# The step behind an output block: second scores ahead of the weighted sums, and differences that end ten products before the block's end

## The chip, the cores and the metric

The kernel runs on one core of one Trainium2 chip. The metric is device microseconds from start to end. The kernel before took 1464.12 us (median of three runs, 1463.6 to 1466.82).

## The reference

Two attention branches read the same input x (2048 rows of 512) and are mixed by a gate. Everything is float32.

```python
g = sigmoid((x * gate_w).sum(-1, keepdims=True))
# branch A: 32 heads of 16, each row looks at 8 rows, 2 apart, behind it
logits = einsum("bhsd,bhswd->bhsw", q, kg) * scale      # masked before row 0
o_a    = einsum("bhsw,bhswd->bhsd", softmax(logits), vg)
# branch B: 32 query heads of 16, one key and one value head, all 2048 keys
scores = einsum("bhqd,bkd->bhqk", q, k) * 16 ** -0.5
o_b    = einsum("bhqk,bkd->bhqd", softmax(scores), v)
return g * (o_a @ A_wo) + (1 - g) * (o_b @ B_wo)
```

## The kernel before, in words

**Units and steps.** Branch B is 4 blocks of 512 queries by 8 groups of 4 heads, 32 units. A unit is 16 steps, one for each 128 keys, so there are 512 steps. Step s does three things. Two pairs of score products (`exp_pair(s, 0)` and `exp_pair(s, 1)`, L471, contraction 64, the two of a pair in the upper and the lower half of the array) fill a bank pair each, `pe0` and `pe1`. ScalarE turns each into 128x1024 exponentials (L477, tile `pexp`). And `weighted(s)` (L486) adds the weighted sums of the values into the bank `po`. A step in the loop issues the scores of s and the weighted sums of s - 1.

**Maxima.** A softmax needs its row maximum before its exponentials, so the maxima of a unit are made some units ahead: 2048 score products of 128x512 whose largest value VectorE takes. They are put wherever there is room, in three forms:

- a pair (`fill_pair`): two products into the bank pair `pm`, one reduction of 128x1024 (L350);
- a single (`fill_one`): one product into `ps` (also called m1) or `po`, one reduction of 128x512 (L362);
- a difference (`fill_diff`, L399, then `fill_sum`): one product with the difference of two key blocks into `pd0` or `pd1`, which ScalarE clamps at zero (L411, tile `dd`); then one product into `ps` or `po`, which VectorE adds to the clamped part and reduces in one instruction (L423). Two of the 2048 products are settled by it.

**Output blocks.** Three times in the loop, `out_phase` multiplies four rows of tiles of the finished branches by the output weights. Each product is split between the upper and the lower half of the array; two streams, one for each half, are issued side by side, and maxima go between them. While a block runs, the bank pair `pm` is split into `pd0` and `pd1`. The block's fourth output lies in `pe1`. At its end `out_store` copies it: ScalarE the upper half's sum (L685), then VectorE the lower half's (L686), both into the tile `two`; GpSimd adds the two (L692). Until both copies are done, `pe1` can take no new scores.

**Order.** Each engine works through its instructions in the order written. That order comes from a planner that runs while the kernel is built. It keeps a clock for each engine and a time at which each bank is free, and issues a filler if its bank is free within a slack. In `stream`, which plans a block, `closing` is true near the end: no new differences then. At the same point, once the first scores of step s are out, `rejoin` makes `pd0` and `pd1` the pair `pm` again, which takes the second scores of s (`exp_pair(s, 1, m2, "m2")`). The set `led` holds the three steps s that a block stood in; the step behind such a block has an order of its own.

The page's lines that this text speaks of, beside those above: L803 is the block's product, L643 and L645 prepare a row of tiles, L652 and L659 to L663 turn one, L689 copies an output inside the block.

Of the kernel before, what the change touches and what calls it, by code (L numbers as in the profile page):

```python
# [41 lines left out]
LEAD, M2S, M1S, MARGIN = 1.75, 0.5, 0.3, 0.12  # L42
# [6 lines left out]
def gated_mix_kernel(ctx, tc, xt, wa, wk, wq, wo_a, wo_b, out):  # L49
# [21 lines left out]
    m1 = pp.tile([P, 512], F32, name="ps")  # L71
    po = pp.tile([P, 512], F32, name="po")
    pp2, m2 = None, None
# [230 lines left out]
    free = {"m1": 0.0, "e0": 0.0, "e1": 0.0, "po": 0.0, "d0": 24.0, "d1": 24.0}  # L304
# [89 lines left out]
    def paired():  # L394
        return len(slots) > 1 and slots[0][3] % 2 == 0 and slots[0][3] // 2 in formed and slots[1] == slots[0][:3] + (slots[0][3] + 1,) and fillable()
# [20 lines left out]
    def room(b, slack):  # L416
        return len(pend[b]) < len(held[b]) and read_d[b][turn_of[b] % len(held[b])] <= clk["pe"] + slack

    def fill_sum(b, dst, key):
        v, pr, t, kc, k, ready = pend[b].pop(0)  # L420
        m = unit_tile(v)
        max_mm(dst, v, pr, t, kc + 1, b)
        got = nc.vector.tensor_tensor_reduce(held[b][k], dst, held[b][k], 1.0, -FMAX, ALU.add, ALU.max, m[:, b, pr, t, kc:kc + 1])  # L423
        free[key] = read_d[b][k] = after("dve", max(after("pe", 0, T_R) + T_LAT, ready), T_TTR) + 0.08
        mark(got, free[key])
        filled(v, 2)

    def fill_odd(b, dst, key):
        got = next((h for h in half if h[4] == b), None)
        if got is None:  # L430
            v, pr, t, kc = slots.pop(0)
            got = (v, pr, t, kc, b)
            half.append((v, pr, t, kc, 1 - b))
        else:
            half.remove(got)
        half.insert(0, got)
        fill_one(dst, key)
# [26 lines left out]
    pe, pexp, exped, homes = [], {}, {}, []  # L464
# [230 lines left out]
    def fits(key, slack=-MARGIN):  # L695
        return key in free and free[key] <= clk["pe"] + slack and not (wanted and key in ("d0", "d1"))

    def side_fill(b, closing):
        now = clk["pe"]
        dst, key = ((m1, "m1"), (po, "po"))[b]  # L700
        if pend[b]:
            if fits(key) and pend[b][0][5] <= now + 0.7 and clk["dve"] <= now + 1.5:
                return lambda: fill_sum(b, dst, key)
            if len(pend[b]) == len(held[b]):
                return None
        single = not pend[b] and fits(key) and clk["dve"] <= now + 1.4
        if any(h[4] == b for h in half):
            return (lambda: fill_odd(b, dst, key)) if single else None
        if todo[b] or paired() and len(todo[1 - b]) < 2:
            if fits(f"d{b}") and room(b, 1.2) and clk["act"] <= now + 2.2 and clk["dve"] <= now + 2.6 and not closing:  # L710
                return lambda: fill_diff(b, apart[b], f"d{b}")
            if todo[b] and single:
                return lambda: plain(b, dst, key)
        elif slots and fillable() and single and not paired():
            return lambda: fill_odd(b, dst, key)
        return None
# [8 lines left out]
    def plain(b, dst, key):  # L725
        if todo[b]:
            v, pr, t, kc = todo[b].pop(0)
            half.extend([(v, pr, t, kc, b), (v, pr, t, kc + 1, b)])
        fill_odd(b, dst, key)

    apart = []
# [9 lines left out]
    def stream(seq, mm, done, s):  # L741

        nonlocal pp2
        at, told = [0, 0], 0
        ready = free.pop("m2")
        pp2.release()
        pp2 = tc.alloc_tile_pool(name="parts", bufs=1, space=PSUM)
        if len(held[0]) < 2:
            more = p1x[0].tile([P, 2, 512], F32, name="dd2", tag="qx", bufs=1)
            for b in range(2):  # L750
                held[b].append(more[:, b])
                read_d[b].append(0.0)
        apart[:] = [pp2.tile([P, 512], F32, name=f"pd{k}") for k in range(2)]
        free["d0"] = free["d1"] = ready
        free["po"] = 1e9
        cl = [clk["pe"]] * 2
        while min(at) < len(seq) or any(pend):
            if free["po"] > 1e8 and min(at) > 3 and max(cl) > exped[s - 1] + 0.1:
                clk["pe"] = max(cl)
                weighted(s - 1)  # L760
                finish_a((s - 1) // NJ, nc.gpsimd)
                free["po"] = clk["dve"] + 0.1
                cl = [clk["pe"]] * 2
            if apart and max(at) > len(seq) - 6 and s in exped and max(free["d0"], free["d1"]) <= max(cl):
                clk["pe"] = max(cl)
                rejoin()
                exp_pair(s, 1, m2, "m2")
                cl = [clk["pe"]] * 2
            b = int(cl[1] < cl[0])
            clk["pe"] = cl[b]  # L770
            do = side_fill(b, max(at) > len(seq) - 6)
            if do:
                do()
                cl[b] += T_R
            elif at[b] < len(seq) and at[b] <= at[1 - b] + 2:
                dur = mm(b, seq[at[b]])
                cl[b] = clk["pe"] + dur
                at[b] += 1
            else:
                cl[b] += 0.07  # L780
            clk["pe"] = cl[b]
            while told < min(at):
                told += 1
                done(seq[told - 1])
        plain_todo()
        clk["pe"] = max(cl)
        if apart:
            rejoin()
            exp_pair(s, 1, m2, "m2")
# [93 lines left out]
    def fill_ready(key, slack):  # L883
        if fillable() and free[key] <= clk["pe"] + slack:
            clk["pe"] = max(clk["pe"], free[key])
            if key == "m1":
                fill_one()
            elif half and (not slots or half[0][0] < slots[0][0] or slots[0][0] >= len(stacked)):
                fill_one(m2[:, 0, :], "m2")
            elif slots:  # L890
                fill_pair(m2, "m2")
            return True
# [365 lines left out]
    outs, due, led = 0, [], set()  # L1258
    for s in range(NS + 1):
        u, kt = divmod(s, NJ)  # L1260
        if len(stacked) < NU and s >= max(2, 16 * (gone(len(stacked)) + 1)):
            stack(len(stacked))
        if s < NS and kt == 0 and u not in shifted:
            while u not in shifted:
                clk["pe"] += 0.5
                run_tasks()
                if u not in shifted and left.get(u, 1):
                    assert pause(4)
        v = min(x[0][0] for x in (half, slots, [(NU,)]) if x)
        need = left.get(v, NF // NU)  # L1270
        steps = 16 * v - 6 - s
        short = need - 2.8 * max(0, steps) if v < NU else 0
        lead = (NF - to_go()) / 64 - s / 16
        order = (0, "m2", "m1", 1) if s > 1 else (1, "m2", "m1", 0) if s else ()
        if s - 1 in led:
            order = (0, "m2", "m1", "po", 1)
        k, n = outs // 4, C - (outs >= NJ - 4)
        if outs == NJ - 4:
            if short > 0 and steps < 2:
                pause(short)  # L1280
        elif due or outs < NJ and outs // NH in done and kt == 15 and NHG * (k + 1) - 1 in shaped and (lead < LEAD or s >= 16 * (NHG * (k + 2) + 1) - 1):
            if not due:
                prepare(outs, n)
                due.append(n)
            else:
                out_phase(list(range(outs, outs + 4)), due.pop(), s)
                outs += 4
                led.add(s)
                order = ()
        elif short > 0 and steps < 2:  # L1290
            pause(short)

        for which in order:
            if which == "m2":
                if slots or half:
                    fill_ready("m2", M2S)
                else:
                    next(tail, None)
            elif which == "m1":
                if singles(s) and fill_ready("m1", M1S):  # L1300
                    owing[0] -= 1.0
            elif which == "po":
                weighted(s - 1)
            elif s < NS:
                exp_pair(s, which)
        if s - 1 in exped:
            weighted(s - 1)
            if kt == 0 and s < NS:
                finish_a(u - 1, nc.gpsimd)
        run_tasks()  # L1310
        run_pool()
# [79 lines left out]
```

## Time and profile before

| what | value |
|---|---|
| median of three runs | 1464.12 us |
| the profiled execution's own time | 1463.92 us |
| its span in the trace | 1462.1 us |
| TensorE busy | 1448.2 us (99%) |
| ScalarE busy | 1292.0 us (88%) |
| VectorE busy | 1141.9 us (78%) |
| GpSimd busy | 954.6 us (65%) |
| share of TensorE in the chain that ended last | 92% |
| output blocks | about 845 to 880, 1144 to 1176 and 1275 to 1308 us |

In rows of instructions in order of time, the columns are the start, the time from the first start to the last end, engine, line, operation, tiles with shapes and how many; in brackets the idle time of that engine before the row, and what ended it. A matmul of 512 columns lasts about 0.39 us, but the next starts after 0.12 to 0.24 us, so how long TensorE needs for a piece of work is read from start to start. In rows of stretches of time each engine has its busy microseconds and count, and PEclk is the granted clock, 1.00 at full speed.

### The profile page before, as it was taken

How to read it: one execution, taken by the hardware profiler on the slowest of the kernel's cores; microseconds unless marked ns; L12 is line 12 of the kernel's file. 1: busy time of each engine (PE TensorE's matmuls, PEld its weight loads, DVE VectorE, ACT ScalarE, POOL GpSimd, SP SyncE). 2: the span in 40 equal slices, each digit the busy share in tenths (PEclk: the TensorE clock that was granted, in tenths of full speed). 3: DMA queues.
4: the chain of work that ended last, by engine and by line, in shares of the span. 5: the costliest groups of instructions: out<-in, count | busy, mean ns of one | idle time of the engine just before them, and what ended most of it. 6: DMA issues, size and time to landing. Idle time of an engine off the chain costs nothing.

```text
span 1462.1 us, 29622 instructions
## 1 busy us (share of the span) xinstructions
PE 1448.2 (99%) x10989; PEld 743.1 (51%) x10989; DVE 1141.9 (78%) x1857; ACT 1292.0 (88%) x1649; POOL 954.6 (65%) x1714
## 2 busy tenths in 40 slices
PE   9999999999999999999999999999999999999999
PEld 6899999833333333333333373333333743373335
DVE  6888888788887888888888876888888778778821
ACT  5788888699999999999999988999999889879994
POOL 6951888888979898898898897888881211130000
PEclk9999999999999999999999999999999999999999
DMA  6652442411202111012022020211200000000000
GB/s 225 171 159 72 146 129 89 136 49 41 79 12 79 47 44 68 31 39 78 17 74 72 13 93 8 82 42 42 71 12 13 27 16 1 2 31 1 1 2 29
DMA packets 45688, 85.70 MB, mean 59 GB/s; under 512 B 10400, under 2 KB 28248, under 8 KB 41448
## 3 DMA queue, kind: packets, MB, share of 16 engines
q1 hardware_dynamic: 38552, 45.21, 10.0%
q0 software_dynamic: 6560, 37.95, 7.8%
q8 instruction: 86, 1.41, 0.4%
q10 hardware_dynamic: 432, 0.66, 0.1%
q14 instruction: 58, 0.48, 0.1%
HBM read 57.97 MB, written 25.25 MB: 57 GB/s over the span
## 4 chain that ended last, share of the span: by engine, by line
PE 92%; POOL 2%; ACT 2%; DVE 1%; issue 1%; DMA 1%; SPq 0%; POOLq 0%; ACTq 0%; DVEq 0%
PE po L486 34%; PE pe L471 24%; PE pf L1109 9%; PE pm L328 8%; PE ps L328 5%; PE pe L803 5%; PE pd L399 3%; PE po L328 1%; PE pe L1320 1%; ACT pexp L477 1%; DMA ad<-stage 1%; POOL xl L82 1%; DVE mx L350 1%; DMA xraw<-xt 0%; PE pf L195 0%
## 5 line engine op out<-in xcount | busy, mean ns | idle before, releaser
L477 ACT ACTIVATE pexp<-pe 128x1024 f32<-128x1024 f32 x1021 | 983.4, 1023 | 64.4 <-PE pe L471 61.1
L350 DVE TENSOR_REDUCE mx<-pm 128x2 f32<-128x1024 f32 x470 | 574.0, 1221 | 178.1 <-PE pm L328 174.4
L486 PE MATMUL po<-pexp,vst 128*32 128x512 f32 x4096 | 546.4, 605 | 4.5 <-DVE mx L423 3.3
L471 PE MATMUL pe<-qst,kst 64*128 64x512 f32 x1914 | 492.6, 459 | 2.0 <-ACT pexp L477 2.0
L471 PEld LDWEIGHTS pe<-qst,kst 64*128 64x128 f32 x1914 | 193.5, 184 | 437.0 <-ACT pexp L477 408.6
L411 ACT ACTIVATE dd<-pd 128x512 f32<-128x512 f32 x384 | 224.5, 601 | 50.7 <-PE pd L399 24.7
L362 DVE TENSOR_REDUCE mx<-ps 128x1 f32<-128x512 f32 x309 | 209.8, 679 | 3.4 <-PE pe L803 2.0
L328 PE MATMUL ps<-kst,qst 62*128 62x512 f32 x475 | 194.2, 409 | 0.2
L549 POOL TENSOR_TENSOR pr<-aext 128x256 f32<-128x256 f32 x256 | 181.9, 740 | 4.2 <-DMA aext<-ad 4.0
L328 PE MATMUL pm<-kst,qst 62*128 62x512 f32 x880 | 178.7, 397 | 0.5 <-ACT pexp L477 0.2
L609 POOL TENSOR_TENSOR oa<-oa,av 128x256 f32<-128x256 f32 x224 | 164.1, 733 | 15.8
L486 PEld LDWEIGHTS po<-pexp,vst 128*32 128x32 f32 x4096 | 80.6, 108 | 171.7 <-issue 157.2
L423 DVE CUSTOM_DVE_ANT_0 dd<-ps,dd 128x512 f32<-128x512 f32 x193 | 133.0, 689 | 25.8 <-PE ps L328 7.8
L423 DVE CUSTOM_DVE_ANT_0 dd<-po,dd 128x512 f32<-128x512 f32 x191 | 131.6, 689 | 22.6 <-PE po L328 10.2
L1109 PE MATMUL pf<-wal,xh 64*128 64x384 f32 (+1 forms) x496 | 148.3, 337 | 0.0
L399 PE MATMUL pd<-kd,qst 62*128 62x512 f32 x372 | 146.4, 398 | 1.7 <-ACT dd L411 1.7
L606 POOL TENSOR_TENSOR av<-aext,lg 128x256 f32<-128x256 f32 x224 | 139.4, 622 | 12.6
L1109 PE MATMUL pf<-wah,xh 64*128 64x384 f32 (+1 forms) x496 | 145.7, 338 | 0.0
L1109 PE MATMUL pf<-wah,xl 64*128 64x384 f32 (+1 forms) x496 | 142.3, 337 | 0.0
L328 PEld LDWEIGHTS ps<-kst,qst 62*128 62x128 f32 x475 | 87.8, 185 | 33.7 <-DVE mx L362 25.6
L513 POOL TENSOR_TENSOR rl<-rl,gate_t 128x16 f32<-128x16 f32 x31 | 7.1, 230 | 143.3 <-DVE rl L506 143.1
L1109 PEld LDWEIGHTS pf<-wal,xh 64*128 64x128 f32 x496 | 90.7, 186 | 0.3
(210 smaller groups left out, 1817.6 us busy)
## 6 DMA issues: line engine op xcount, KB each, us to landing
aext<-ad POOLq DMA_DIRECT2D x32, 1056.0 KB, 5.4
ad<-stage SPq DMA_DIRECT2D x32, 384.0 KB
qst<-qd SPq DMA_DIRECT2D x60, 128.0 KB
xraw<-xt SPq DMA_DIRECT2D x16, 256.0 KB
qd<-qhi SPq DMA_DIRECT2D x16, 256.0 KB
qd<-qlo SPq DMA_DIRECT2D x16, 256.0 KB
qst<-qd SPq DMA_DIRECT2D x60, 64.0 KB
qst<-ml SPq DMA_DIRECT2D x212, 2.0 KB
```

Source lines behind the costliest of these rows:

```text
L328: nc.tensor.matmul(dst, qst[place(v)][b:b + 62, pr, t * P:(t + 1) * P], kst[b:b + 62, kc * 512:(kc + 1) * 512], start=True, stop=True)
L350: got = nc.vector.tensor_reduce(m[:, :, pr, t, kc], dst, AX.X, ALU.max)
L362: got = nc.vector.tensor_reduce(m[:, odd, pr, t, kc:kc + 1], dst, AX.X, ALU.max)
L399: nc.tensor.matmul(dst, qst[place(v)][b:b + 62, pr, t * P:(t + 1) * P], kd[0][b:b + 62, kc // 2, :], start=True, stop=True)
L411: got = nc.scalar.activation(held[b][k], dst, AF.Relu)
L423: got = nc.vector.tensor_tensor_reduce(held[b][k], dst, held[b][k], 1.0, -FMAX, ALU.add, ALU.max, m[:, b, pr, t, kc:kc + 1])
L471: nc.tensor.matmul(bank[:, odd, :], kst[b:b + 64, kt * P:(kt + 1) * P], qst[place(u)][b:b + 64, pr, :], start=True, stop=True)
L477: got = nc.scalar.activation(e, bank, AF.Exp, scale=SCALE)
L486: nc.tensor.matmul(po[32 * i:32 * i + 32, :], vst[:, kt, :], pexp[s, i // 2][:, i % 2, :], start=(kt == 0), stop=(kt == NJ - 1))
L549: nc.gpsimd.tensor_mul(pr[:, k], q, e[:, o:o + NH, AC:2 * AC])
L609: nc.gpsimd.tensor_add(ao, ao, av)
L1109: inst = nc.tensor.matmul(home(x)[0][:, :n], l[h], r[h], start=(i == 0 and b == 0), stop=(i == 3 * C - 1 and b == 1))
```

## The change

Two numbers in `stream` and one order in the loop. The differences end, and `pm` is joined again, ten products before a block's end, where it was six. In the step behind a block the order was first scores, pair, single, weighted sums, second scores. It is now first scores, single, second scores, pair, weighted sums; the pair there may be issued with a slack of 1.2 us, where it was 0.5.

```diff
-            if apart and max(at) > len(seq) - 6 and s in exped and max(free["d0"], free["d1"]) <= max(cl):
+            if apart and max(at) > len(seq) - 10 and s in exped and max(free["d0"], free["d1"]) <= max(cl):
...
-            do = side_fill(b, max(at) > len(seq) - 6)
+            do = side_fill(b, max(at) > len(seq) - 10)
...
         if s - 1 in led:
-            order = (0, "m2", "m1", "po", 1)
+            order = (0, "m1", 1, "m2", "po")
...
-                    fill_ready("m2", M2S)
+                    fill_ready("m2", 1.2 if s - 1 in led else M2S)
```

The instructions move as follows. In the names, `pe_4202` is `pe0`, `pe_4203` is `pe1`, and `qst`, `kst`, `woh`, `wol` are queries (in a block, prepared rows), keys and output weights. TensorE near the end of the first block, the difference of the two orders:

```order
 L803 MATMUL pe_4203<-woh_4273,qst_84 128x512 x5
 L328 MATMUL ps<-kst,qst_79 128x512
-L803 MATMUL pe_4203<-woh_4273,qst_84 128x512
-L399 MATMUL pd_9839<-kd,qst_79 128x512
-L803 MATMUL pe_4203<-wol_4274,qst_84 128x512
-L803 MATMUL pe_4203<-woh_4273,qst_84 128x512
-L471 MATMUL pe_4202<-qst_82,kst 128x512 x2
-L399 MATMUL pd_9840<-kd,qst_79 128x512
+L803 MATMUL pe_4203<-woh_4273,qst_84 128x512 x2
+L471 MATMUL pe_4202<-qst_82,kst 128x512 x2
+L471 MATMUL pm<-qst_82,kst 128x512 x2
```

The last two differences (L399) are gone, and the second scores of s, which went into `pm` one product before the end, now stand right behind the first.

TensorE from the end of the first block, before:

```order
L803 MATMUL pe_4203<-woh_4273,qst_84 128x512 x4
L471 MATMUL pm<-qst_82,kst 128x512 x2
L803 MATMUL pe_4203<-woh_4273,qst_84 128x512
L328 MATMUL po<-kst,qst_79 128x512
L471 MATMUL pe_4202<-qst_82,kst 128x512 x2
L328 MATMUL ps<-kst,qst_79 128x512
L486 MATMUL po<-pexp,vst 32x512 x4
L471 MATMUL pe_4203<-qst_82,kst 128x512 x2
L471 MATMUL pe_4202<-qst_82,kst 128x512 x2
L328 MATMUL pm<-kst,qst_79 128x512 x2
L471 MATMUL pe_4203<-qst_82,kst 128x512 x2
```

The same place now:

```order
L803 MATMUL pe_4203<-woh_4273,qst_84 128x512 x8
L471 MATMUL pe_4202<-qst_82,kst 128x512 x2
L328 MATMUL ps<-kst,qst_79 128x512
L471 MATMUL pe_4203<-qst_82,kst 128x512 x2
L328 MATMUL pm<-kst,qst_79 128x512 x2
L486 MATMUL po<-pexp,vst 32x512 x4
L471 MATMUL pe_4202<-qst_82,kst 128x512 x2
L328 MATMUL pm<-kst,qst_79 128x512 x2
L471 MATMUL pe_4203<-qst_82,kst 128x512 x2
```

The weighted sums of s have moved behind the second scores of s + 1 and a pair of maxima, and the late sum into `po` (L328) is no longer ahead of them. The second and the third block end in the same nine rows now, up to one single more behind the second `pm`.

VectorE at the end of the first block, before (L423 prints a second row for the value it leaves):

```order
L423 ISA dd,mx<-ps,dd 128x512
L423 ISA mx 128x1
L686 COPY two<-pe_4203 128x512
L423 ISA dd_9838,mx<-po,dd_9838 128x512
L423 ISA mx 128x1
L362 TENSOR_REDUCE mx<-ps 128x1
L350 TENSOR_REDUCE mx<-pm 128x2 x2
```

And now:

```order
L423 ISA dd,mx<-po,dd 128x512
L423 ISA mx 128x1
L686 COPY two<-pe_4203 128x512
L362 TENSOR_REDUCE mx<-ps 128x1
L350 TENSOR_REDUCE mx<-pm 128x2 x3
```

No sum into `po` stands behind the copy any more. Over the whole kernel there are six differences fewer (L399 and L411, 384 of L411 become 378; L423 likewise), four pairs more (L350, 470 to 474) and four singles more (L362, 335 to 339). TensorE issues as many matmuls as before.

## The prediction

> **What bounds the kernel now.** I read the chain of waits first, then TensorE in the loop and at the three block ends, in order of time. The chain by engine, and one stretch of the loop:
>
> ```profile
> PE 92%; POOL 2%; ACT 2%; DVE 1%; issue 1%; DMA 1%; SPq 0%; POOLq 0%; ACTq 0%; DVEq 0%
> ```
>
> ```profile
> 890.00:930.00 40.00, 40.00 (x287) 14.79 (x289) 32.75 (x41) 37.86 (x43) 30.63 (x59) 1.00 0.14 38
> ```
>
> The five pairs of numbers behind the length are TensorE, weight loads, VectorE, ScalarE and GpSimd. In the loop TensorE has no idle time, VectorE is at 82% and ScalarE at 95%. So a step costs what its matmuls cost:
>
> ```profile
> 895.96 0.50 PE L471 MATMUL pe<-qst,kst 64*128 64x512 f32 x2
> 896.30 0.40 PE L328 MATMUL pm<-kst,qst 62*128 62x512 f32 x2
> ...
> 896.87 1.07 PE L486 MATMUL po<-pexp,vst 128*32 128x512 f32 x8
> 897.86 0.50 PE L471 MATMUL pe<-qst,kst 64*128 64x512 f32 x2
> ...
> 898.43 0.40 PE L328 MATMUL ps<-kst,qst 62*128 62x512 f32 x1
> ...
> 899.99 0.50 PE L471 MATMUL pe<-qst,kst 64*128 64x512 f32 x2
> ```
>
> From start to start, a step without a single is 1.90 us (895.96 to 897.86) and one with a single 2.13, so a single costs 0.23. First scores take 0.34 and weighted sums 0.99.
>
> TensorE does stand still behind each block. The first block's end, on TensorE, ScalarE and VectorE:
>
> ```profile
> 879.13 0.39 PE L803 MATMUL pe<-woh,qst 64*128 64x512 f32 x1
> 879.17 0.40 PE L328 MATMUL po<-kst,qst 62*128 62x512 f32 x1
> 879.37 0.43 PE L471 MATMUL pe<-qst,kst 64*128 64x512 f32 x2
> 879.67 0.50 PE L328 MATMUL ps<-kst,qst 62*128 62x512 f32 x1
> 882.42 1.94 PE L486 MATMUL po<-pexp,vst 128*32 128x512 f32 x8 [2.25 <-DVE mx L423]
> 884.28 1.22 PE L471 MATMUL pe<-qst,kst 64*128 64x512 f32 x4
> 885.30 0.47 PE L328 MATMUL pm<-kst,qst 62*128 62x512 f32 x2
> 886.19 0.49 PE L471 MATMUL pe<-qst,kst 64*128 64x512 f32 x2 [0.43 <-ACT pexp L477]
> ```
>
> ```profile
> 879.43 1.03 ACT L477 ACTIVATE pexp<-pm 128x1024 f32<-128x1024 f32 x1 [0.82 <-PE pm L471]
> 880.35 0.59 ACT L685 ACTIVATE two<-pe 128x512 f32<-128x512 f32 x1
> ```
>
> ```profile
> 880.97 0.69 DVE L686 COPY two<-pe 128x512 f32<-128x512 f32 x1 [1.36 <-ACT two L685]
> 881.58 0.68 DVE L423 CUSTOM_DVE_ANT_0 dd<-po,dd 128x512 f32<-128x512 f32 x1
> ```
>
> This is one queue of four. The last product starts at 879.13, but ScalarE first makes the exponentials of `pm` (issued late, just ahead of it), then its copy at 880.35; VectorE's copy waits for that one, and the last sum into `po` stands behind the copy; only then may the weighted sums write `po`, at 882.42. The clock then drops:
>
> ```profile
> 880.00:882.00 2.00, 0.17 (x1) 0.00 (x0) 1.03 (x2) 1.86 (x3) 0.50 (x2) 1.00 0.00 0
> 882.00:884.00 2.00, 1.58 (x8) 0.23 (x8) 0.87 (x3) 0.00 (x0) 1.94 (x6) 0.51 0.10 30
> 884.00:886.00 2.00, 1.77 (x10) 0.83 (x6) 0.19 (x1) 0.88 (x1) 2.00 (x4) 0.64 0.30 110
> ```
>
> The second block's end, TensorE and then ScalarE, and the third's:
>
> ```profile
> 1173.97 0.95 PE L803 MATMUL pe<-wol,qst 64*128 64x512 f32 x6
> ...
> 1175.92 0.39 PE L803 MATMUL pe<-woh,qst 64*128 64x512 f32 x1
> ...
> 1176.23 0.56 PE L471 MATMUL pe<-qst,kst 64*128 64x512 f32 x2
> 1177.96 1.06 PE L486 MATMUL po<-pexp,vst 128*32 128x512 f32 x8 [1.18 <-ACT pexp L477]
> 1178.96 0.73 PE L471 MATMUL pe<-qst,kst 64*128 64x512 f32 x4
> 1179.52 0.40 PE L328 MATMUL pm<-kst,qst 62*128 62x512 f32 x2
> 1179.76 0.39 PE L328 MATMUL ps<-kst,qst 62*128 62x512 f32 x1
> 1180.57 0.50 PE L471 MATMUL pe<-qst,kst 64*128 64x512 f32 x2 [0.42 <-ACT pexp L477]
> ```
>
> ```profile
> 1173.83 1.03 ACT L477 ACTIVATE pexp<-pe 128x1024 f32<-128x1024 f32 x1 [1.24 <-PE pe L471]
> ...
> 1176.40 0.60 ACT L685 ACTIVATE two<-pe 128x512 f32<-128x512 f32 x1 [0.57 <-issue]
> 1176.89 1.02 ACT L477 ACTIVATE pexp<-pm 128x1024 f32<-128x1024 f32 x1
> ```
>
> ```profile
> 1307.25 0.47 PE L803 MATMUL pe<-woh,qst 64*128 64x512 f32 x2
> ...
> 1310.49 1.07 PE L486 MATMUL po<-pexp,vst 128*32 128x512 f32 x8 [1.10 <-DVE mx L423]
> ...
> 1313.11 0.49 PE L471 MATMUL pe<-qst,kst 64*128 64x512 f32 x2 [0.39 <-ACT pexp L477]
> ```
>
> **What the ends cost now.** I take the time from the last product to the second scores of s + 2 (the rows with idle of about 0.4) and subtract the matmuls between them at their pace at full clock: weighted sums 1.00, two pairs of scores back to back 0.56 (1178.96 to 1179.52), a pair of maxima 0.24, a single 0.23, the product itself 0.24, first scores 0.24.
> - First: 886.19 - 879.13 = 7.06; work 0.24 + 0.24 + 0.23 + 1.00 + 0.56 + 0.24 = 2.51; lost 4.55. Of this 1.32 is the clock: weighted sums 1.86 for 1.00, two pairs of scores 1.02 for 0.56.
> - Second: 4.65; work 0.31 (to 1176.23) + 0.24 + 1.00 + 0.56 + 0.24 + 0.23 = 2.58; lost 2.07.
> - Third: 5.86; work as in the second, with 0.24 for the product, and a pair, a single and half a slot for the sum besides, 3.10; lost 2.76.
>
> Together 9.38 us.
>
> **The ends after the change.** Call the start of the last product T. The exponentials of `pm` now follow at once on those of the first scores, ten products early: in the second block from 1173.83 + 0.92 to about 1175.8, before ScalarE's copy can start, so that ScalarE is free when the last product is done. The copy then starts at T + 0.48, as it did in the second block, where ScalarE was idle (1175.92 to 1176.40). With 0.60 for it, 0.03 until VectorE begins (880.94 to 880.97), 0.69 for VectorE's copy and about 0.10 to TensorE (0.05 to 0.15 in the three ends), the second scores of s + 1 start at T + 1.90. Meanwhile TensorE has the product, the first scores and a single, 0.71 of work. Then scores 0.34, pair 0.24, weighted sums 1.00 (the sums into `po` are long reduced, the exponentials of s long there), first scores 0.34: the next pair would be due at T + 3.82. VectorE reduces the first pair from its matmuls' end, T + 2.24 + 0.40, for 1.22, so that the next starts near T + 3.95 and the second scores of s + 2 at T + 4.2. They find their exponentials done, since those of s + 1 start near T + 2.4. Work in this is 2.87, so 1.35 is lost a block, 4.05 in all. The gain is 9.38 - 4.05 = 5.33.
>
> **What else moves.** The moved steps issue matmuls and one exponential, no DMA; GpSimd's addition and the store follow the copies and come earlier. By the order, twelve products leave the differences for four more pairs and four singles. In the blocks nine matmuls go (six L399, two into `ps`, one into `po`); two streams start one each 0.11 (0.95 less 0.39, over five), at 0.12 with fillers, which saves 1.06. The loop gets four pairs at 0.24 and, net, one single at 0.23: 1.19. Cost 0.13, in steps where TensorE is the bound. VectorE and ScalarE cover theirs, since they have room in the loop. The maxima that come later belong to a unit four units ahead, over 100 us, and the order has no filler pause for them; no wait there.
>
> **Sum.** 5.33 - 0.13 = 5.2 us less. The profiled execution took 1463.92, of which its span is 1462.1; that becomes 1458.7. The median was 0.2 higher, so I forecast 1458.9. Bounds: if the copies chain faster (copy at the product's end, T + 0.39, no wait for the pair) the loss is 1.0 a block instead of 1.35, and with the 0.13 free the sum is 1457.7; the third block's waits are the least certain, another 0.5, so 1457.2. The upper end is the first rival's.
>
> **Rivals.**
> - *The clock drops behind every wait.* TensorE's new idle is from the single's end (T + 0.48 + 0.39) to T + 1.90, 1.0 us. Idle of 1.18 and 1.10 left the next weighted sums at 1.06 and 1.07, full pace; 2.25 did not. By the nearest rows no drop follows. If it does, each costs the 1.32 of the first block: 1458.9 + 3 x 1.32 = 1462.9. 12%.
> - *The drop behind the first block has another cause than the wait* and stays: 1458.9 + 1.3 = 1460.2. For it: only one of three waits shows a drop. Against it: the drop follows the longest. 6%. [...]
> - *The wait only changes its place.* The second scores need `pe1`, and so both copies. If ScalarE's copy still comes behind a late exponential, the wait for `pe1` is as long as that for `po` was, and 9.38 stays: 1464.3. It decides if the exponentials of `pm` end after T + 0.48; I have 0.25 us to spare in the second block. 10%.
> - *Slower: VectorE sets the pace.* Differences are its cheapest way to two maxima:
>
> ```profile
> L350 DVE TENSOR_REDUCE mx<-pm 128x2 f32<-128x1024 f32 x470 | 574.0, 1221 | 178.1 <-PE pm L328 174.4
> L362 DVE TENSOR_REDUCE mx<-ps 128x1 f32<-128x512 f32 x309 | 209.8, 679 | 3.4 <-PE pe L803 2.0
> L423 DVE CUSTOM_DVE_ANT_0 dd<-ps,dd 128x512 f32<-128x512 f32 x193 | 133.0, 689 | 25.8 <-PE ps L328 7.8
> ```
>
>   Four pairs at 1.221 and four singles at 0.679 for six sums at 0.689 are 3.5 us more of it. Were it the bound from block to block, that would come on top and nothing be gained: 1467.6. It decides where VectorE's share of a loop stretch reaches 100%; it is 82%, and 174.4 of its 178.1 us idle ahead of L350 wait for TensorE. 6%.
>
> **How the numbers follow.** The forecast has the remaining 66%, with 1457.2 to 1461.2 as its own range. A measurement of this kernel can tell about 0.2%, 2.9 us, from no change: faster is below 1461.2. That takes in the forecast (less 2% for a loss a block of 2 us) and the second rival, 70%; same has the first, the third and those 2%, 24%; slower the last, 6%. From 1457.2 to 1462.9 lie the forecast and the first two rivals, 84%.
>
> **What would show it.** Right: behind each block the row of second scores, not of weighted sums, has the idle time, about 1.0 us, released by VectorE's copy L686; the weighted sums follow without idle, in 1.06; no stretch with a clock of 0.51 near 880; ScalarE's copy starts about 0.5 behind the last product; the later waits of 0.4 for exponentials are gone; 474 of L350, 378 of L411. Wrong: a copy that waits for exponentials, a drop of the clock, steps in the loop above 1.90 and 2.13, or idle of TensorE elsewhere.

## The result

The changed kernel takes 1461.03 us (median of ten runs, 1460.15 to 1461.97) against 1465.39 for the kernel before on the same chip (ten runs). The ratio is 0.9973, with a 95% interval from 0.9965 to 0.9981: 2.8 to 5.1 us less. 1458.9 was forecast, 5.2 less. The time lies in the forecast's own range (1457.2 to 1461.2), close to its upper end, and the gain is smaller than forecast. Beside the experiments, the kernel before took 1463.5 us (median of 12 executions) where its granted clock was 1.000, 1464.8 (13) at 0.999, 1466.2 (15) at 0.998 and 1467.1 (9) below, while all ten executions of the changed kernel had 1.000.

The chain of waits after, by engine, and two groups of its page:

```profile
PE 92%; POOL 2%; ACT 2%; DVE 1%; DMA 1%; issue 1%; SPq 0%; POOLq 0%; ACTq 0%; DVEq 0%
...
L486 PE MATMUL po<-pexp,vst 128*32 128x512 f32 x4096 | 545.5, 605 | 0.0
L471 PE MATMUL pe<-qst,kst 64*128 64x512 f32 x1914 | 494.1, 459 | 3.7 <-DVE two L686 3.1
```

The weighted sums (L486) no longer wait; they had 4.5 us of idle time ahead of them. In their place the scores (L471) have 3.7 us, 3.1 of them until VectorE's copy L686. The first block's end, on TensorE, ScalarE and VectorE (the last of the six products in the first row starts at 879.61):

```profile
879.13 0.87 PE L803 MATMUL pe<-woh,qst 64*128 64x512 f32 x6
879.84 0.39 PE L471 MATMUL pe<-qst,kst 64*128 64x512 f32 x2
880.07 0.40 PE L328 MATMUL ps<-kst,qst 62*128 62x512 f32 x1
881.46 0.50 PE L471 MATMUL pe<-qst,kst 64*128 64x512 f32 x2 [1.00 <-DVE two L686]
881.80 0.40 PE L328 MATMUL pm<-kst,qst 62*128 62x512 f32 x2
882.13 1.07 PE L486 MATMUL po<-pexp,vst 128*32 128x512 f32 x8
883.12 0.50 PE L471 MATMUL pe<-qst,kst 64*128 64x512 f32 x2
883.52 0.50 PE L328 MATMUL pm<-kst,qst 62*128 62x512 f32 x2
883.86 0.40 PE L471 MATMUL pe<-qst,kst 64*128 64x512 f32 x2
```

```profile
878.66 1.01 ACT L477 ACTIVATE pexp<-pm 128x1024 f32<-128x1024 f32 x1
880.09 0.60 ACT L685 ACTIVATE two<-pe 128x512 f32<-128x512 f32 x1 [0.41 <-POOL tr L555]
```

```profile
880.72 0.69 DVE L686 COPY two<-pe 128x512 f32<-128x512 f32 x1 [1.01 <-ACT two L685]
```

ScalarE is done with `pm` at 879.67, before its copy starts at 880.09. (The releaser named for the copy is inferred; the copy starts 0.47 to 0.49 behind the last product in all three blocks.) The two copies follow each other, and the second scores start when the second is over. The weighted sums take 1.07, full pace; 2.25 us of idle and the slow stretch are gone. The other two blocks end alike:

```profile
1175.67 0.50 PE L471 MATMUL pe<-qst,kst 64*128 64x512 f32 x2 [1.11 <-DVE two L686]
...
1306.85 0.50 PE L471 MATMUL pe<-qst,kst 64*128 64x512 f32 x2 [1.00 <-DVE two L686]
```

### The profile page after: what moved, and what is told of

Same layout as the page of the kernel before. It is cut to its first block, busy times and chain, and to the rows that moved or that the text cites. A ratio compares the mean times of both kernels' runs of the same rounds, so it can differ in the third digit from the quotient of the medians.

```text
span 1459.2 us, 29601 instructions
## 1 busy us (share of the span) xinstructions
PE 1448.0 (99%) x10989; PEld 743.5 (51%) x10989; DVE 1146.3 (79%) x1853; ACT 1289.5 (88%) x1643; POOL 954.3 (65%) x1714
## 4 chain that ended last, share of the span: by engine, by line
PE 92%; POOL 2%; ACT 2%; DVE 1%; DMA 1%; issue 1%; SPq 0%; POOLq 0%; ACTq 0%; DVEq 0%
PE po L486 33%; PE pe L471 24%; PE pf L1109 10%; PE pm L328 8%; PE ps L328 6%; PE pe L803 4%; PE pd L399 3%; PE po L328 1%; PE pe L1320 1%; DMA ad<-stage 1%; DVE mx L350 1%; ACT pexp L477 1%; POOL pr L549 1%; POOL tr L555 1%; POOL xl L82 0%
## 5 line engine op out<-in xcount | busy, mean ns | idle before, releaser
L350 DVE TENSOR_REDUCE mx<-pm 128x2 f32<-128x1024 f32 x474 | 579.0, 1221 | 172.0 <-PE pm L328 168.7
L486 PE MATMUL po<-pexp,vst 128*32 128x512 f32 x4096 | 545.5, 605 | 0.0
L471 PE MATMUL pe<-qst,kst 64*128 64x512 f32 x1914 | 494.1, 459 | 3.7 <-DVE two L686 3.1
L471 PEld LDWEIGHTS pe<-qst,kst 64*128 64x128 f32 x1914 | 194.8, 183 | 437.9 <-ACT pexp L477 408.1
L411 ACT ACTIVATE dd<-pd 128x512 f32<-128x512 f32 x378 | 220.8, 601 | 49.9 <-PE pd L399 25.6
L362 DVE TENSOR_REDUCE mx<-ps 128x1 f32<-128x512 f32 x313 | 212.7, 680 | 4.4 <-PE ps L328 4.4
L328 PE MATMUL ps<-kst,qst 62*128 62x512 f32 x476 | 194.5, 409 | 0.2
L328 PE MATMUL pm<-kst,qst 62*128 62x512 f32 x886 | 179.9, 398 | 0.3
L486 PEld LDWEIGHTS po<-pexp,vst 128*32 128x32 f32 x4096 | 80.6, 108 | 167.6 <-issue 158.9
L423 DVE CUSTOM_DVE_ANT_0 dd<-ps,dd 128x512 f32<-128x512 f32 x190 | 131.0, 690 | 24.1 <-PE ps L328 7.4
L423 DVE CUSTOM_DVE_ANT_0 dd<-po,dd 128x512 f32<-128x512 f32 x188 | 129.7, 690 | 22.8 <-PE po L328 10.4
L399 PE MATMUL pd<-kd,qst 62*128 62x512 f32 x366 | 144.4, 399 | 1.7 <-ACT dd L411 1.7
L328 PEld LDWEIGHTS ps<-kst,qst 62*128 62x128 f32 x476 | 88.0, 185 | 33.2 <-DVE mx L362 27.4
```

The source lines that it names most:

```text
L328: nc.tensor.matmul(dst, qst[place(v)][b:b + 62, pr, t * P:(t + 1) * P], kst[b:b + 62, kc * 512:(kc + 1) * 512], start=True, stop=True)
L350: got = nc.vector.tensor_reduce(m[:, :, pr, t, kc], dst, AX.X, ALU.max)
L362: got = nc.vector.tensor_reduce(m[:, odd, pr, t, kc:kc + 1], dst, AX.X, ALU.max)
L399: nc.tensor.matmul(dst, qst[place(v)][b:b + 62, pr, t * P:(t + 1) * P], kd[0][b:b + 62, kc // 2, :], start=True, stop=True)
L411: got = nc.scalar.activation(held[b][k], dst, AF.Relu)
L471: nc.tensor.matmul(bank[:, odd, :], kst[b:b + 64, kt * P:(kt + 1) * P], qst[place(u)][b:b + 64, pr, :], start=True, stop=True)
```

## How the traces are compared

Up to the first block's first product all kernels here issue the same matmuls, and yet that product starts anywhere between 845.3 us (before) and 848.5 (a kernel below); 846.2 after. From there on a stretch repeats to 0.15 us between traces of the same order. So I cut each trace by the starts of matmuls: *blocks* from a block's first to its last product; *ends* from there to the weighted sums of s + 1; *loops* the rest up to the last matmul. Each column is the sum over the three.

| kernel | differences | blocks | ends | loops | total |
|---|---|---|---|---|---|
| before | 384 | 98.40 | 18.78 | 496.21 | 613.4 |
| after | 378 | 97.87 | 14.22 | 497.49 | 609.6 |
| order only | 387 | 99.20 | 16.68 | 494.21 | 610.1 |
| ten only | 378 | 97.89 | 12.55 | 497.36 | 607.8 |
| sums first | 378 | 97.96 | 11.69 | 498.13 | 607.8 |
| fourteen | 376 | 97.77 | 13.95 | 498.62 | 610.3 |

The change itself is 3.8 us less by this, of which the ends are 4.56, the blocks 0.53, and the loops 1.28 the other way.

## The experiments

All stand against the kernel before on the same chip; the ratios have 95% intervals.

**The order alone.** The new order behind the block, differences ending six products early.

```diff
-            if apart and max(at) > len(seq) - 10 and s in exped ...
+            if apart and max(at) > len(seq) - 6 and s in exped ...
-            do = side_fill(b, max(at) > len(seq) - 10)
+            do = side_fill(b, max(at) > len(seq) - 6)
```

> The new order behind a block, with the differences ending six products early as before. Theory (behind a block TensorE waits for pe1, so for ScalarE's and then VectorE's copy; the early end of the differences is what lets ScalarE's copy start at once): the exponentials of pm again stand ahead of ScalarE's copy behind the first and the third block, so the second scores wait until about 2.6 us behind the start of the last product instead of 1.86; idle 1.7 to 1.8 us there, no drop of the clock. Lost at the three ends about 6.3 us, against 9.3 before and 4.2 with both parts: 1462 to 1463.5. Rival (the order is the whole gain, the ten products only move maxima about): 1460 to 1461, idle about 1.0 us as with both parts.

1461.71 us, ratio 0.9974 (0.9965 to 0.9983): nearly what both parts reach, against the theory's 1462 to 1463.5. At the first end the second scores start where the theory had them:

```profile
880.68 0.39 PE L803 MATMUL pe<-woh,qst 64*128 64x512 f32 x1
...
883.26 0.50 PE L471 MATMUL pe<-qst,kst 64*128 64x512 f32 x2 [1.55 <-DVE two L686]
883.60 0.39 PE L328 MATMUL pm<-kst,qst 62*128 62x512 f32 x2
883.92 1.49 PE L486 MATMUL po<-pexp,vst 128*32 128x512 f32 x8
```

The second scores start 2.58 behind the last product there and 2.56 at the second end; at the third, where the theory had 2.6 too, it is 1.86. The ends are 2.5 us longer than with both parts, a slow stretch (weighted sums 1.49) included, which I had excluded. The rival's picture, idle of 1.0, is wrong too. What I had not priced is the other side: this kernel has nine differences more, and blocks and loops together are 1.95 us shorter for it (593.41 against 595.36). By the traces ten matmuls more stand in its blocks (1.33 us more, 0.13 each), fourteen fewer in its loops (3.28 less, 0.23 each), and the other four in its ends. So by my estimate a difference given up costs about 0.2 us: two matmuls at 0.12 in the block's two streams become two singles at 0.23 in the loop.

**Ten products alone.** The old order and slack.

```diff
-            order = (0, "m1", 1, "m2", "po")
+            order = (0, "m2", "m1", "po", 1)
-                    fill_ready("m2", 1.2 if s - 1 in led else M2S)
+                    fill_ready("m2", M2S)
```

> The differences end ten products early, with the old order behind the block (first scores, pair, single, weighted sums, second scores) and the old slack. Theory: with pm's exponentials early and no late sum in po, the weighted sums need not wait; they start about 0.95 us behind the last product and fill just the time in which pe1 is copied, so the second scores find it free at about 1.95. Next second scores at 3.5 us behind the last product instead of 4.25: 0.75 us a block less than with both parts, 1458.5 to 1459.5. Rival (the order is the gain): the wait returns in front of the weighted sums, about 1464 to 1465. Rival (the order makes no odds): 1461.

1459.51 us, ratio 0.9963 (0.9951 to 0.9976), at the upper end of the theory's span. The first end:

```profile
882.65 0.39 PE L328 MATMUL ps<-kst,qst 62*128 62x512 f32 x1
882.97 1.07 PE L486 MATMUL po<-pexp,vst 128*32 128x512 f32 x8
883.97 0.74 PE L471 MATMUL pe<-qst,kst 64*128 64x512 f32 x4
884.94 0.51 PE L328 MATMUL pm<-kst,qst 62*128 62x512 f32 x2 [0.23 <-DVE mx L350]
885.58 0.50 PE L471 MATMUL pe<-qst,kst 64*128 64x512 f32 x2
```

Nothing waits ahead of the weighted sums or of the second scores: the sums end just after the copies of `pe1` do (second scores 1.92 to 2.02 behind the last product, where the copies alone let them start at 1.86). With the ten products in place, the old order is the better one, by 1.8 us in the traces; the theory had 2.25.

**Sums first.** A third order with the ten products, and the same once more beside the change.

```diff
-            order = (0, "m1", 1, "m2", "po")
+            order = (0, "m1", "po", 1, "m2")
```

> Ten products, and the order first scores, single, weighted sums, second scores, pair: a third order for the same work. Theory: weighted sums about 0.7 us behind the last product without idle, the second scores wait some 0.15 us for pe1 and the next ones for exponentials until 3.45; one pair less is done by then than in the old order, so 0.24 us a block is owed: 1459 to 1460. Rival (weighted sums behind the second scores are what helps): above 1463.

1458.94 us, ratio 0.9958 (0.9946 to 0.9971). The ends are the shortest of all; the pair that is not done there returns in the loops (498.13), and the total equals that of ten only. What is left is a wait for exponentials:

```profile
880.71 1.06 PE L486 MATMUL po<-pexp,vst 128*32 128x512 f32 x8
881.78 0.49 PE L471 MATMUL pe<-qst,kst 64*128 64x512 f32 x2
882.11 0.40 PE L328 MATMUL pm<-kst,qst 62*128 62x512 f32 x2
882.35 0.40 PE L471 MATMUL pe<-qst,kst 64*128 64x512 f32 x2
883.39 0.50 PE L471 MATMUL pe<-qst,kst 64*128 64x512 f32 x2 [0.65 <-ACT pexp L477]
```

> The change itself once more, beside the next run: 1461.0, idle 1.0 to 1.1 us behind each block.

> Ten products with the weighted sums ahead of the second scores and the pair behind them, once more beside the change itself. Theory (with the ten products the weighted sums need not wait, so they cover the copies): 1.8 us less than the change, as the traces of the two have it from the first block's first product to the last matmul: 1459.2. Rival (the difference came from the part ahead of the first block, which is the same in both): equal to the change.

The change took 1460.86 (0.9973, 0.9962 to 0.9985) and sums first 1459.7 (0.9965, 0.9954 to 0.9977). The intervals overlap; the traces keep them apart, with totals of 609.5 and 607.9. By the traces, both new kernels beat the change; by their intervals, both beat the kernel before.

**One copy.** ScalarE copies the block's last output alone.

```diff
-        if closing:
+        if False:
```

> Both parts of the change, but the block's last output is copied by ScalarE alone in one instruction of 128x1024, as the other outputs of a block are, in place of ScalarE and then VectorE with 128x512 each. Theory (the second scores wait for the two copies in a row): 0.60 + 0.03 + 0.69 become 1.02, so the idle in front of the second scores falls from 1.0 to about 0.7 us, released by ScalarE: 0.9 us less over three blocks, 1460.1. Rival (something else sets that wait): idle stays at 1.0 us, 1461 or, since ScalarE is held 0.42 us longer, up to 1462.3.

```profile
880.60 0.40 PE L328 MATMUL ps<-kst,qst 62*128 62x512 f32 x1
881.70 0.49 PE L471 MATMUL pe<-qst,kst 64*128 64x512 f32 x2 [0.70 <-ACT two L689]
```

The idle is 0.70, released by ScalarE, as forecast. 1460.69 us (0.9967, 0.9954 to 0.9979), 0.7 less than the change in the traces where 0.9 was forecast: the next pair of maxima starts 0.13 late, right behind VectorE's reduction of the pair before.

**Joining late.** The differences end ten early, `pm` may be joined only six early.

```diff
-            if apart and max(at) > len(seq) - 10 and s in exped ...
+            if apart and max(at) > len(seq) - 6 and s in exped ...
```

> Both parts of the change, but pm is joined again, and takes the second scores of s, only six products before a block's end; new differences still end ten before. Theory (of the ten products it is the early exponentials of pm that pay, since they clear ScalarE for its copy; ending the differences early only costs): exponentials of pm end up to 0.5 us behind the point at which ScalarE's copy could start, the second scores of s + 1 start at 2.2 to 2.6 us behind the last product instead of 1.86, at the same number of differences: 1.0 to 2.2 us more over three blocks than with both parts, 1462 to 1463.3. Rival (the end of the differences pays, since no late sum is left): 1461, second scores at 1.86.

1460.98 us (0.997, 0.9961 to 0.9979), the idle 1.0 to 1.1, the trace's total 609.6: the theory's loss is not there.

```profile
877.23 1.03 ACT L477 ACTIVATE pexp<-pe 128x1024 f32<-128x1024 f32 x1 [0.89 <-DVE mx L423]
878.18 1.03 ACT L477 ACTIVATE pexp<-pm 128x1024 f32<-128x1024 f32 x1
879.57 0.60 ACT L685 ACTIVATE two<-pe 128x512 f32<-128x512 f32 x1 [0.36 <-PE pe L803]
```

Even so the exponentials of `pm` end at 879.2, before the copy. Joining six early is early enough. In the kernel before, `pm` was joined one product before the first block's end although six were allowed; by its condition the planner also asks that `pd0` and `pd1` be read, and the last differences held them. So it is their end that pays.

**A longer wait.** ScalarE's copy is repeated one, two and three times behind the three blocks.

```diff
-            nc.scalar.activation(two[:, 0], eb[k][:, 0, :], AF.Copy)
+            for _ in range(1 + j // 4 + 1):
+                nc.scalar.activation(two[:, 0], eb[k][:, 0, :], AF.Copy)
```

> Both parts of the change, with ScalarE's copy repeated once more behind the first block, twice more behind the second and three times more behind the third, so that TensorE's idle time there grows by about 0.5, 1.0 and 1.6 us (1.5, 2.1 and 2.6 instead of 1.0 to 1.1), with the same matmuls in the same order. [...]

One run, 1470.0 us. The stretches of 2 us with the waits and those behind them; the column behind GpSimd's is the clock:

```profile
882.00:884.00 2.00, 0.64 (x4) 0.30 (x4) 1.29 (x2) 1.54 (x3) 0.62 (x1) 1.00 0.00 0
884.40:886.40 2.00, 2.00 (x12) 0.69 (x6) 0.95 (x1) 0.52 (x1) 1.86 (x8) 0.50 0.38 139
1179.00:1181.00 2.00, 0.74 (x8) 0.38 (x12) 1.29 (x2) 1.54 (x3) 0.71 (x1) 1.00 0.01 4
1181.40:1183.40 2.00, 2.00 (x12) 0.83 (x6) 0.86 (x1) 0.51 (x2) 0.26 (x2) 0.50 0.35 131
...
1314.50:1316.50 2.00, 1.79 (x8) 0.70 (x12) 1.28 (x3) 1.24 (x2) 1.77 (x2) 0.50 0.00 0
```

Idle of 1.68, 2.41 and 2.95 us, where 1.5, 2.1 and 2.6 were expected: the clock is at 0.50 behind all three, for 3.41 us each time by the trace's clock records.

**Two tiles.** VectorE's copy goes to a tile of its own.

```diff
-            nc.vector.tensor_copy(two[:, 1], eb[k][:, 1, :])
+            own = p2b[0].tile([P, D], F32, name="twob", bufs=1)
+            nc.vector.tensor_copy(own, eb[k][:, 1, :])
```

> Both parts of the change, and VectorE's copy of the block's last output goes to a tile of its own instead of the second half of ScalarE's; GpSimd adds the two. Theory (VectorE's copy waits for ScalarE's only since both write the tile two): both copies start about 0.5 us behind the last product, the second scores at about 1.25 instead of 1.86, idle 0.4: 1.8 us less over three blocks, 1459.2. Rival (VectorE waits for ScalarE for another reason, such as both reading the bank pair pe1): the two copies still follow each other, 1461.

1460.92 us (0.997, 0.9958 to 0.9981), idle 1.0 as before: the theory fell, the shared output tile is not what orders the copies.

```profile
880.51 0.69 DVE L687 COPY twob<-pe 128x512 f32<-128x512 f32 x1 [1.01 <-ACT two L685]
```

**No upper half.** So the next theory is the other thing that both touch, the bank pair `pe1`.

```diff
-            nc.scalar.activation(two[:, 0], eb[k][:, 0, :], AF.Copy)
+            nc.scalar.activation(two[:, 0], kst[:, 0:512].bitcast(F32), AF.Copy)
```

> Both parts of the change, but ScalarE's copy at the block's end takes 128x512 of the keys instead of the upper half's sum in pe1, so a quarter of the output rows of the three blocks (each block's last output) lacks that half. Theory (VectorE's copy waits for ScalarE's only since both read the bank pair pe1): VectorE's copy starts about 0.5 us behind the last product, the second scores at about 1.25 instead of 1.86, idle 0.4; the same sequence of matmuls otherwise, so up to 1.8 us less: 1459.2. Rival (VectorE's copy takes until 1.80 for another reason): idle 1.0 as with both parts, 1461.

```profile
880.48 0.40 PE L328 MATMUL ps<-kst,qst 62*128 62x512 f32 x1
881.25 0.50 PE L471 MATMUL pe<-qst,kst 64*128 64x512 f32 x2 [0.37 <-DVE two L686]
```

It holds: idle 0.37 to 0.56, the second scores 1.23 to 1.34 behind the last product, 1459.41 us (0.9963, 0.995 to 0.9977), 1.2 us less than the change in the traces. Both copies only read `pe1`, each its own bank, and still the second is ordered behind the first. That order stands in the semaphores of the program as built: in the change VectorE's copy waits for the semaphore that ScalarE's copy raises, also with two tiles, and without the upper half it does not. Whether the chip would need it was not tried.

**Fourteen products** in place of ten.

```diff
-            if apart and max(at) > len(seq) - 10 and s in exped ...
+            if apart and max(at) > len(seq) - 14 and s in exped ...
-            do = side_fill(b, max(at) > len(seq) - 10)
+            do = side_fill(b, max(at) > len(seq) - 14)
```

> Both parts of the change with fourteen in place of ten. By the order one pair and two differences fewer and six singles more than with ten. The waits behind the blocks are as with ten (the exponentials of pm were early enough): second scores at 1.86. Theory (moved maxima cost what they cost in the loop): four matmuls less in the blocks at 0.12, six singles more at 0.23 to 0.25 and a pair less at 0.24 in the loop, 0.7 to 0.8 us more: 1461.8. Rival (they cost more than their slots, as the step from six to ten did, by half as much again): 1462.3 or more.

1462.5 us (0.9983, 0.9973 to 0.9992). The second scores stay at 1.86. The trace's total is 0.8 above the change's, as the theory had it; the median is 1.5 above, on the rival's side. Either way the four products more cost and bring nothing.

## Why the prediction was right, and where not

- **What bounds the ends:** right. The chain (copy 0.48 behind the last product, VectorE's 0.03 behind ScalarE's, second scores at 1.90) was measured as 0.48, 0.03 and 1.86, within 0.01, in all three blocks; one copy and no upper half moved the wait as that chain says.
- **The ends after the change:** right. 1.35 us lost a block were forecast; to the second scores of s + 2 it is 4.26, 4.27 and 4.25, less the work of 2.87, 1.39. Together 9.38 became 4.17, for 4.05 forecast. (The third block's 5.86 starts at the first of the two products in its row; the last one starts at 1307.33, so 9.38 should be 9.30.) The late waits of 0.4 are gone.
- **The clock:** right for the change, but closer than I wrote. I took 1.18 without and 2.25 with a drop as the ends; order only shows one behind 1.55. And the forecast took one drop of 1.32 us as given, as in its one trace. The one drop of that trace gives a granted clock of 0.999; the other executions of the kernel before have 1.000 in 12 and 0.998 or less in 24, so I take it that some have no drop and others several. Reckoned from 1463.5 at a granted clock of 1.000, the change gains about 2.5 us; the other 1.9 of the 4.4 between the medians would then be drops that it no longer has. Forecast were 3.9 and 1.3. That the sum comes as near to 5.2 as 4.4 is partly luck; from the one trace to the other it is 3.8.
- **The moved maxima, "Cost 0.13":** the step that failed. By the prediction's own terms the ends were to change by -4.91 (their work grows by 0.42), the blocks by -1.06 and the loops by +0.77. Measured are -4.56, -0.53 and +1.28. In the blocks I counted nine matmuls less, but the two late sums into `po` behind the first and the third block lie in the ends, where I had them already, and the third block got no shorter (32.45 to 32.58). In the loops, the third has three singles more, 25 to 28, and 0.85 us. The first has 75 singles before and after, and two products more into `pm`: 0.24 at the prediction's price, but about 0.1 by its own steps (one with a single product into `pm` took 2.07 for 2.13). It is 0.52 longer. There I had said that TensorE is the bound and that VectorE and ScalarE cover their share, which holds on average only. Two exponentials in a row take 1.94 us from the first's start to the second's end, about as long as a step without a single. Where two such steps follow each other, the scores can come up against them:

```profile
976.21 0.40 PE L328 MATMUL pm<-kst,qst 62*128 62x512 f32 x2
976.45 0.40 PE L471 MATMUL pe<-qst,kst 64*128 64x512 f32 x2
976.78 1.07 PE L486 MATMUL po<-pexp,vst 128*32 128x512 f32 x8
977.78 0.50 PE L471 MATMUL pe<-qst,kst 64*128 64x512 f32 x2
978.11 0.40 PE L328 MATMUL pm<-kst,qst 62*128 62x512 f32 x2
978.41 0.49 PE L471 MATMUL pe<-qst,kst 64*128 64x512 f32 x2
978.84 1.06 PE L486 MATMUL po<-pexp,vst 128*32 128x512 f32 x8
```

```profile
977.34 1.02 ACT L477 ACTIVATE pexp<-pe 128x1024 f32<-128x1024 f32 x1
```

  The second scores at 978.41 start right behind the exponential that reads their bank (977.34 + 1.02), 0.30 behind the pair where it was 0.24, and the weighted sums follow 0.43 behind them where it was 0.33: the step takes 2.06 for 1.90. In the first loop, four such steps without a single are 0.15 us or more too long after the change, and one before, so this is about 0.5 us. (A step of 2.25 near 1115 stands in both kernels.) In the third loop a step with a single takes 2.41 for 2.13, which none did before; there the pair starts at 1344.47, 0.52 behind the first scores in place of 0.34, right behind VectorE's reduction of the pair before it (L350, 1343.20 to 1344.42).

  These readings are from the traces; no run tests them.
- **The two parts:** the prediction credited them together, and did not see how they stand to each other: alone they give 3.3 and 5.6 us in the traces, together 3.8. The early end takes away what the weighted sums waited for; then they cover the copies, and the new order only moves them from where they cover.
- **The rivals:** the wait did change its place, from 2.25, 1.18 and 1.10 to 1.00, 1.11 and 1.00, but only in the first block did it become much shorter. The third rival's price, everything stays, is refuted by the ends. VectorE is at 82% of the first loop (210.98 of 257.70 us), 81% before, and sets no pace there as a whole; the single step above is the exception that I found.

## What to carry to other kernels

When a bank must be copied out before it can be written again, put the longest piece of work that needs neither the bank nor the copies into that time. Removing what that piece waited for may be worth more than moving it away (here 5.6 us alone against 3.3, in the traces); price both parts apart. And price a filler by what its slot costs where it goes: here half a slot between two streams (0.12 us), a whole one in a loop that has room for no more (0.23).

## What the runs showed of the hardware

At the blocks' ends TensorE's clock halved for 3.41 us behind 1.55 us of idle time (order only), 2.25 (before) and 1.68, 2.41 and 2.95 (the longer wait), and kept full speed behind 1.10 and 1.18 (before) and 1.00, 1.11 and 1.00 (after). I had expected the bound between 1.18 and 2.25. In the traces of before, of order only and of the longer wait the first drop came 877.23 us after the clock first rose to full speed, which is 257 times 3.413 us, the length of a drop in the clock records; the later stretches at full speed up to the next drop (293.55 and 129.71 us with the longer wait) are 86 and 38 times that. In the 3.41 us ahead of each of these five drops TensorE was idle for 1.55 to 2.66 us; before, it was 1.86.

Idle time alone gives no clean bound, though. With ten products alone, TensorE waits 1.65 us in an earlier part of the kernel, longer than the 1.55 above. It is idle for 1.59 of the 3.41 us in the row below, and the clock stays at 1.00:

```profile
183.29:186.70 3.41, 1.82 (x18) 1.78 (x20) 0.99 (x5) 2.42 (x5) 3.10 (x14) 1.00 0.40 117
```

```profile
184.88 0.49 PE L399 MATMUL pd<-kd,qst 62*128 62x512 f32 x1 [1.65 <-ACT dd L411]
```

Nine executions of the kernel before had a granted clock of 0.996 or 0.997, as three drops give (the longer wait has three and 0.996), so its shorter waits, 1.10 and 1.18 us, may bring one as well; no trace here shows it. What decides besides the idle time, these runs do not show.
